# A delta-rule attention feeding an MLP: weights and joins in another order, chunk 0's moves ahead of a block read, chunk 1's second update two pieces later

## The chip, the cores and the metric

The kernel runs on one core of one Trainium2 chip. The metric is the device time of one execution in microseconds (us), and of several executions the median. Besides, one execution of each kernel is recorded by the hardware profiler; all durations of single instructions come from that one.

## What is computed

Two stages, joined by a transposition. The first is the delta rule: per batch and head (4 and 8 of them) a 48 × 48 state is read and corrected token by token, over 768 tokens. The second is an MLP on the 3,072 rows of 384 values that this gives: a product with `w_in` (384 × 2048), x · sigmoid(x), and a product with `w_out` (2048 × 384). All is float32.

```python
for t in range(S):                      # B, H, S, D = 4, 8, 768, 48
    kt, vt, bt = k_n[:, :, t], v[:, :, t], beta[:, :, t, None]     # k_n: keys of length 1
    y[:, :, t] = einsum('bhd,bhde->bhe', q[:, :, t], state)
    v_old = einsum('bhde,bhd->bhe', state, kt)
    state = state + bt[..., None] * einsum('bhd,bhe->bhde', kt, vt - v_old)
...
x = y.transpose(0, 2, 1, 3).reshape(B * S, H * D)
h = x @ w_in
out = (h * (1 / (1 + exp(-h)))) @ w_out
```

## The kernel before

**The tiling.** The 768 tokens are cut into six chunks of 128 and each chunk into two halves of 64. For a half, the token-by-token recurrence becomes a small triangular system for each batch and head: scores of keys against keys and queries against keys, the inverse of a 64 × 64 triangle, a product with the corrected values, an update of the state, and the outputs. The inverse is built from 32 × 32 blocks, which VectorE inverts in 31 steps for all batches and heads at once ("rank", L628). The blocks go out to DRAM and come back in that other layout: the read is `block_in` (L581–583), whose tile is `g`. Then TensorE joins two 32 × 32 inverses to a 64 × 64 one, in many products of 32 × 32: a "corner" (L718), a "turned" product (L734), a "straight" one (L747) and a "merge" (L807). Each of these is done for batches 0 and 1 and for batches 2 and 3.

**The names in the trace.** `pt` (L501) is a transposition of keys or queries on TensorE (four for one batch), evacuated by VectorE or ScalarE. `pa` (L530) are scores; VectorE's mask (L540, `above`) evacuates those of queries. `pl`, `px` and `py` belong to the joins. `ph` (L829) and `pz` (L841) are the steps before the update `pu` (L861). `pyc` (L909 and L922) holds the outputs of a half, one bank for batches 0 and 1 (g = 0) and one for batches 2 and 3 (g = 1). `phid` (L1049) is the hidden layer of the MLP, and `po`, `px` and `py` at L1084 and L1156 its output.

**From outputs to the MLP.** `even_heads` (L930 on) brings a `pyc` bank into the layout of `xT`, where heads and their 48 values lie along the 128 partitions. Every bank is copied once as a whole to `part` (48 × 512). The even heads are then copied from `pyc` to `xT`, six copies of 48 × 128 for each bank, on ScalarE (`by_act`, L545) or VectorE (`by_dve`, L548). The odd heads need other partitions and go from `part` to `xT` by DMA; these are the "moves", collected in a list and issued on SyncE's queue by `move()` (L902). The first phid of a half waits for all of them.

**The MLP's pieces.** The MLP is written as a list of pieces. A piece of the hidden layer is a *run*: six matmuls of 128 × 128 by 128 × 256 into half of a `phid` bank. `run(n)` issues the next n pieces. A run needs its slab of `w_in` (256 columns) narrowed to the type that the products use; `fill` ("f") issues a narrowing, which is spread over ScalarE (L232), VectorE (L237, L241) and POOL (L245).

**The loads.** The DMAs that SyncE issues stand in one list (`line`), which keeps the order of the program. A slab of `w_in` is three DMAs of 256 KB (`fetch_w_in`, L278–293). `deep(...)` makes a load wait until the last but one DMA of the list has landed, so that two are under way at a time. The raw slabs go to rooms that are free at that time. Slab 7 goes into `sums_of_g`, where the queries of chunk 1 lie until they are transposed.

**The order of the work.** Each engine executes in program order, and the program order of everything around the change is written by hand: a text of words (the call of `script`, L1549), read from left to right. A letter stands for a step and the number behind it for how often:

| word | step |
|---|---|
| `s` | next step of `solve(0)`, then of `solve(1)` |
| `j` | next piece of the joins of half 1 (`rest`) |
| `T`, `q` | transposition of chunk 1's keys, queries of the next batch |
| `r`, `f` | run of the MLP; narrowing of the next slab of weights |
| `p` | next step of `prepare(1)`: scores of chunk 1 and their blocks' way out and back |
| `i` | next steps of the inverse of chunk 1's blocks (VectorE) |
| `b`, `e`, `l`, `m`, `t`, `w`, `W` | begin a narrowing early; lengths of keys of chunk 1 (`l`) and chunk 2 (`m`); sums of weights; fetches of weights |

Behind the text a loop over the chunks (L1553 on) takes the rest: for c = 1 it ends `solve(1)`, then goes through `prepare(2)`, whose first step are the 16 transpositions of chunk 2's keys, with runs between the steps.

`solve(0)` ends with the update and the outputs of the second half, the copies to `xT` (`copy_out`) and the moves. `solve(1)` ends with `made(1, 1)`: update, outputs, moves and copies of the second half.

Of the kernel before, what the change touches and what calls it, by code (L numbers as in the profile page):

```python
# [19 lines left out]
def kernel(  # L20
# [10 lines left out]
    nc = tc.nc  # L31
    B, H, S, D = q.shape
# [8 lines left out]
    T = 32  # L41
# [48 lines left out]
    def in_line(dma):  # L90

        if line:
            behind(dma, line[-1])
        if pace or depth:
            behind(dma, pace.pop() if pace else line[-2], Sync)
        line.append(dma)
        return dma
# [12 lines left out]
    def together(*parts):  # L110
        for _ in zip_longest(*parts):
            pass
# [63 lines left out]
    def deep(fetch, *args):  # L176

        depth.append(True)
        fetch(*args)
        depth.pop()  # L180
# [397 lines left out]
                ap[rows].rearrange("s u h t -> s (u h) t")[:, :, cols], c == 0 and j % 2 == 1,  # L578
            )

    def block_in(c):  # L581
        there, g, _ = blocks[c]
        in_line(nc.sync.dma_start(out=g, in_=there[:]))

# [313 lines left out]
    def move():  # L900
        for to, of in moves:
            in_line(nc.sync.dma_start(out=to, in_=of))  # L902
        moves.clear()
# [13 lines left out]
    def new(c, g, hf):  # L917

        py = pys.pop(g)
        for u, p, e, _, _, to in of_heads():  # L920
            rows = on(e, hf, g)
            yield pin(nc.tensor.matmul(  # L922
                py[to, C * p + W * u : C * p + W * (u + 1)], lhsT=zbuf[rows, g * HB + u, hf, p, 0:D],
                rhs=aps[c, g][1][rows, u, 2 * p + e, :], start=False, stop=True, skip_group_check=True,
            ))
        copies.append(even_heads(c, g, hf, py))
        go(copies[-1])
# [3 lines left out]
    def even_heads(c, g, hf, py):  # L931

        xT, half = x_half(c, g, hf)
        if g == 0:
            parts[c, hf] = work.tile([P, 2, NP, C], FP32, name="part", tag="x", bufs=1)
        part = parts[c, hf][:, g]
        by = by_dve if c == 1 and hf == 0 and g == 1 else by_act
        by(part[0:D], py[0:D].rearrange("p (a t) -> p a t", a=NP))
        if c == 0:
            yield  # L940
        for h in chained(range(1, H, 2), range(0, H, 2)):
            if c > 0 and h == 0:
                yield
            f = D * h
            while f < D * (h + 1):
                n, at = min(D * (h + 1) - f, P - f % P), W * (1 - h % 2) + f - D * h
                while h % 2 == 0 and (n > T and at % W or f % P % W and n > T):
                    n = T
                to = xT[f % P : f % P + n, f // P, half]
                if h % 2 == 1:  # L950
                    if g == 1:
                        moves.append((
                            xT[f % P : f % P + n, f // P].rearrange("p (g t) -> p g t", g=2),
                            parts[c, hf][at : at + n, :, h // 2, :],
                        ))
                else:
                    by(to, py[at : at + n, C * (h // 2) : C * (h // 2 + 1)])
                f += n
        yield

    def copy_out():
        together(copies.pop(0))
# [18 lines left out]
    def solve(c):  # L981

        if c == 0:
            together(inner(0, 0, 0, CC))
            together(inner(0, 1, 0, M))
            yield
            first_outputs(0)
            yield
            first_outputs(1)
            yield  # L990
            together(update(0, 0, 0), update(0, 1, 0))
            yield
            together(keys(0, 0, 1), keys(0, 1, 1))
            yield
            together(inner(0, 0, 1), old(0, 0, 1))
            yield
            together(inner(0, 1, 1), old(0, 1, 1))
            yield
            together(update(0, 0, 1), update(0, 1, 1))
            yield  # L1000
            together(new(0, 0, 1), new(0, 1, 1))
            copy_out()
            copy_out()
            move()
            yield
            return
        together(merge(c, 0, False), merge(c, 1, False))
        yield
        together(keys(c, 0, 0), keys(c, 1, 0))
        yield  # L1010
        together(merge(c, 0, True), merge(c, 1, True))
        yield
        for hf in range(2):
            if hf == 1:
                together(keys(c, 0, 1), keys(c, 1, 1))
                if c > 1:
                    follow(c)
                yield
            for g in range(2):
                together(inner(c, g, hf), old(c, g, hf))  # L1020
            if hf == 1:
                if c == 1:
                    follow(c)
                load_v(c + 1)
            yield
            made(c, hf)
            yield
            copy_out()
            if hf == 0:
                yield  # L1030
# [184 lines left out]
    def feed_forward(c, hf):  # L1215

        yield from hidden(c, hf)
        yield from combine(c, hf)
# [126 lines left out]
        first_score(b)  # L1345
    busy(1)
    fetch_w_in(2)
    deep(load_q, 1)
    fetch_w_in(4)
    deep(fetch_w_in, 3)  # L1350
    deep(fetch_w_in, 6)
    deep(fetch_w_in, 5)
    begin(("in", 0))
    inv = invert_first(step)

# [82 lines left out]
    def prepare(c):  # L1438

        def evacuate(j, e, to, of):  # L1440
            if j == 1:
                mask(to, of)
            else:
                by_act(to, of)

        def scored(b):
            if b == 0:
                block_room(c)
            score(c, b, (0, 1), (A, CC), evacuate)
            if b % HB == 1:  # L1450
                block_out(c, b // HB)

        if in_blocks(c):
            for g in range(2):
                size(c, g)
            if c == 2:
                yield
                for b in range(B):
                    turn(c, b, 0, (A, CC)[b % 2], True)
            for g in range(2):  # L1460
                for b in range(HB * g, HB * (g + 1)):
                    turn_blocks(c, b, 1)
                yield
            for b in range(B):
                scored(b)
            block_in(c)
            yield
            return
        block_room(1)
        for b in range(B):  # L1470
            score(1, b, (0,), (CC, CC), evacuate)
            if b % HB == 1:
                block_out(1, b // HB)
            yield
        block_in(1)
        yield
        for b in range(B):
            score(1, b, (1,), (A, CC), evacuate)
            yield
# [67 lines left out]
                pieces = chained(feed_forward(1, 0), feed_forward(1, 1))  # L1547

    for text in (  # L1549
        "s f s f T f q T s q T j5 j4 j8 j8 f j5 f q r T j20 j5 j8 j4 j16 j5 j4 b r q r f j4 j4 f W7 r b j4 f2 j4 j4 j32 r f e j6 j6 b j8 j4 f j4 j20 f j4 r j4 j99 l h f2 b l s w2 f r2 l p r s l w3 r p r l p f l2 f l3 b l f l2 s l f l p l3 r l3 s l f l r l2 p f s2 l2 H f l4 f r2 f p2 v l g G r i p i p f r i r i2 r i r i b l i r f r i r b r2 i b b b i2 r2 i2 f b i5 r6 f r f r i2 r2 f r i r f r f i4 f i b r2 i3 b f b f r i r i f k r f r z i b r s r2 t z s b r2 b s m2 r5 t f t m f t m2 r s t m r b s b m r m2 s r m r m r c m2 s m r m t b m2 s m2 b m f m2 t r t m3 r m s m",  # L1550
    ):
        script(text)
    for c in range(1, NCH):  # L1553
        if c > 1:
            solving = solve(c)
            for n in range(9):
                go(solving)
                run(((2, 2, 2, 2, 1, 1, 2, 2, 2), (2, 2, 2, 1, 1, 2, 2, 2, 2))[c == NCH - 1][n])
                if n == 5:
                    pieces = chained(pieces, feed_forward(c, 0), feed_forward(c, 1))  # L1560
        assert next(solving, 0) == 0
        go(long_2, 99)
        if c + 1 < NCH:
            ready = prepare(c + 1)
            for _ in range(3 if c == 1 else 2):
                go(ready)
                run(2)
            step = block_steps(c + 1)
            go(ready)
            run(8 if c > 1 else 6)  # L1570
            for n, _ in enumerate(invert(c + 1, step)):
                run(int(n % 4 != 3 and n != 24))
                if n == 3:
                    load_k(c + 2)
                    if in_blocks(c + 2):
                        load_blocks(k, c + 2, ALL)
            after = lengths(c + 2) if c + 2 < NCH else iter(())
            for _ in range({1: 8, NCH - 2: 10}.get(c, 10)):
                run()
                go(after, 4)  # L1580
            go(after, 99)
# [31 lines left out]
```

## Time and profile before

| | |
|---|---|
| three runs | 639.70, 640.12 and 642.98 us; median 640.12 |
| the profiled execution | 646.08 us, of which the span of the trace is 644.3 |
| mean granted clock of TensorE in it | 0.973 |
| TensorE's matmuls | 623.5 us, 97% of the span |
| VectorE, ScalarE, GpSimd (POOL) | 401.2, 217.2 and 94.3 us |
| costliest group | phid, L1049: 1152 matmuls, 259.6 us |

How to read it: the busy share of an engine is a mean over stages. TensorE ("PE") executes matmuls and weight loads ("PEld") in two overlapping streams. The view by lines gives, for each group of like instructions, the busy time, the mean of one in ns, and the idle time ahead of the group with what ended it ("<-"). "issue" stands for time in which an engine waited for nothing that the profile shows. The view by time gives rows of consecutive like instructions: start (us from the span's start), length, engine, line, operation, tiles and shapes, and in brackets the wait ahead. The view by windows gives, for each stretch, its length, the busy time and count of PE, PEld, DVE, ACT and POOL, the granted clock of TensorE (1 is full speed), the share of time that the DMA engines are busy, and the GB/s that they move.

### The profile page before, as it was taken

Reading aid. Unit: us, or ns where it says so; the run is one execution under the profiler, and the core shown is the slowest. Engines: PE = TensorE matmul, PEld = TensorE weight load, DVE = VectorE, ACT = ScalarE, POOL = GpSimd, SP = SyncE. Lnnn points to the kernel's source line nnn. Section 1 sums busy time; section 2 is a strip of 40 time slices with the busy share of each in tenths; the row PEclk is TensorE's granted clock in tenths of the full one; section 3 lists DMA queues with packets and bytes.
Section 4 is the critical chain, followed back from the end, with each engine's and each line's share of the span. In section 5 each row is a group of like instructions: output and inputs, shape, how many; then the busy total and the mean of one; then the engine's idle time right before and its main releaser. Section 6 shows DMA issues by size and latency. Waiting matters only on the chain.

```text
span 644.3 us, 21893 instructions
## 1 busy us (share of the span) xinstructions
PE 623.5 (97%) x9642; PEld 550.1 (85%) x9642; DVE 401.2 (62%) x917; ACT 217.2 (34%) x512; POOL 94.3 (15%) x96
## 2 busy tenths in 40 slices
PE   6879999999999999999999999999999999999997
PEld 4677787756789988999989989989989989889997
DVE  5845688988865986563987563987464974212112
ACT  2655656151342122451122451122451122441120
POOL 5332630237011020010020010020001000000000
PEclk9759799999999999999999999999999999999999
DMA  9755445170278433268434268334173033100101
GB/s 190 164 141 163 146 97 132 50 148 3 58 150 145 62 85 50 54 133 136 70 79 55 47 137 138 69 79 56 26 154 76 9 79 48 40 14 1 25 0 25
DMA packets 141695, 53.69 MB, mean 83 GB/s; under 512 B 113296, under 2 KB 135056, under 8 KB 141600
## 3 DMA queue, kind: packets, MB, share of 16 engines
q1 hardware_dynamic: 141264, 52.14, 40.2%
q8 instruction: 76, 1.25, 0.8%
q10 hardware_dynamic: 336, 0.15, 0.1%
q14 instruction: 19, 0.16, 0.1%
HBM read 39.62 MB, written 10.49 MB: 78 GB/s over the span
## 4 chain that ended last, share of the span: by engine, by line
PE 92%; DMA 2%; issue 2%; DVE 1%; ACT 1%; SPq 1%; POOL 0%; DVEq 0%; POOLq 0%
PE phid L1049 39%; PE px L1156 16%; PE py L1156 12%; PE po L1084 7%; PE pa L530 3%; PE pz L841 2%; PE ph L829 2%; PE pyc L922 2%; PE pu L861 2%; PE pyc L909 2%; PE pt L501 1%; DMA kb<-in_k_dram 1%; DMA xT<-part 1%; PE px L783 1%; PE py L783 1%
## 5 line engine op out<-in xcount | busy, mean ns | idle before, releaser
L1049 PE MATMUL phid<-xT,w_in 128*128 128x256 f32 x1152 | 259.6, 383 | 2.5 <-DMA xT<-part 1.5
L1049 PEld LDWEIGHTS phid<-xT,w_in 128*128 128x128 f32 x1152 | 217.2, 191 | 33.6 <-issue 4.1
L1059 ACT ACTIVATE gT<-phid 128x512 f32<-128x512 f32 x88 | 52.6, 598 | 147.1 <-PE phid L1049 138.5
L628 DVE SCALAR_TENSOR_TENSOR rank<-g,step,x 128x31 f32<-128x31 f32 (+15 forms) x124 | 49.7, 401 | 36.9 <-DMA g<-blocks 33.4
L1138 DVE TENSOR_TENSOR sums_of_g<-gT 128x384 f32<-128x384 f32 (+1 forms) x60 | 29.8, 516 | 56.5 <-ACT gT L1059 46.0
L1156 PE MATMUL py<-w_out,sums_of_g 128*128 128x192 f32 x320 | 56.8, 329 | 0.0
L1156 PE MATMUL px<-sums_of_w,sums_of_g 128*128 128x192 f32 x320 | 56.6, 329 | 0.0
L1156 PEld LDWEIGHTS px<-sums_of_w,sums_of_g 128*128 128x128 f32 x320 | 52.2, 190 | 0.5
L1156 PEld LDWEIGHTS py<-w_out,sums_of_g 128*128 128x128 f32 x320 | 52.2, 190 | 0.4
L633 DVE TENSOR_TENSOR x<-x,rank 128x31 f32<-128x31 f32 (+15 forms) x124 | 42.5, 343 | 4.3
L468 POOL TENSOR_TENSOR vf<-vf,n_slot 128x768 f32<-128x768 f32 x10 | 14.9, 1490 | 167.9 <-DMA vf<-in_v_dram 121.8
L868 DVE TENSOR_TENSOR state<-state,pu 48x384 f32<-48x384 f32 x44 | 24.3, 552 | 21.9 <-PE pu L861 20.9
L545 ACT COPY xT<-pyc 48x128 f32<-48x128 f32 (+2 forms) x126 | 32.7, 260 | 1.7
L489 DVE STREAM_TRANSPOSE kq<-stage 128x512 f32<-128x512 f32 x28 | 28.2, 1112 | 3.9 <-DMA stage<-in_q_dram 3.8
L1156 PE MATMUL px<-sums_of_w,gT 128*128 128x192 f32 x160 | 28.4, 329 | 0.0
L1156 PE MATMUL py<-w_out,gT 128*128 128x192 f32 x160 | 28.4, 329 | 0.0
L1156 PE MATMUL px<-w_out,gT 128*128 128x192 f32 x160 | 28.0, 327 | 0.0
L841 PEld LDWEIGHTS pz<-vf,xi 64*64 64x64 f32 x768 | 25.2, 142 | 3.2 <-issue 2.6
L551 POOL COPY g<-x 64x256 f32<-64x256 f32 x4 | 5.0, 1242 | 152.5 <-DVE x L636 152.5
L1156 PEld LDWEIGHTS px<-w_out,gT 128*128 128x128 f32 x160 | 26.4, 190 | 0.6
L841 PE MATMUL pz<-vf,xi 64*64 64x48 f32 x768 | 26.9, 226 | 0.0
L1156 PEld LDWEIGHTS py<-w_out,gT 128*128 128x128 f32 x160 | 26.1, 190 | 0.3
(197 smaller groups left out, 831.1 us busy)
## 6 DMA issues: line engine op xcount, KB each, us to landing
vf<-in_v_dram SPq DMA_DIRECT2D x48, 96.0 KB, 3.1
out_dram<-o SPq DMA_DIRECT2D x42, 96.0 KB, 2.2
w_out<-in_moe_w_in_dram SPq DMA_DIRECT2D x12, 256.0 KB, 3.5
sums_of_w<-in_moe_w_out_dram SPq DMA_DIRECT2D x8, 384.0 KB, 4.4
blocks<-ap SPq DMA_DIRECT2D x40, 64.0 KB, 1.9
g<-blocks SPq DMA_DIRECT2D x5, 512.0 KB, 3.7
kb<-in_k_dram SPq DMA_DIRECT2D x12, 192.0 KB, 4.4
kb<-in_k_dram SPq DMA_DIRECT2D x24, 96.0 KB, 4.5
```

The source lines that it names most:

```text
L489: pin(nc.vector.transpose(out=kqs[c, b][:, :, j, :].rearrange("p a (i m) -> p a m i", i=T), in_=src.rearrange("p a (m d) -> p a m d", d=D) ...
L530: pin(nc.tensor.matmul(pa[e][half, p * n * W : (p + 1) * n * W], lhsT=kq[rows, p, 0, half], rhs=kq[rows, p, js[0] : js[-1] + 1, half], sta ...
L545: return pin(nc.scalar.copy(to, of))
L628: pin(nc.vector.scalar_tensor_tensor(out=tv, in0=g[:, 0:m, m : m + 1].to_broadcast([P, m, n]), scalar=step[:, m : m + 1], in1=x[:, m : m + ...
L633: yield pin(nc.vector.tensor_tensor(out=x[:, 0:m, m:T], in0=x[:, 0:m, m:T], in1=tv, op=ALU.add))
L841: yield pin(nc.tensor.matmul(pz[rows, n * D : (n + 1) * D], lhsT=xis[g][rows, u * H + 2 * p + e, :], rhs=vfs[c][rows, hf, g * HB + u, p, : ...
L868: pin(nc.vector.tensor_tensor(out=to, in0=to, in1=by_heads(pu[of]), op=ALU.add))
L1049: pin(nc.tensor.matmul(ph[:, j * GT : (j + 1) * GT], lhsT=w_in[:, a, (2 * f + j) * P : (2 * f + j + 1) * P], rhs=xTs[c, hf][:, a, :], star ...
L1059: pin(nc.scalar.activation(out=hidden_of(c, hf, f), in_=ph[:], func=ACTF.Silu, scale=-0.5 if in_blocks(c) else 0.5))
L1084: pin(nc.tensor.matmul(pos[i][:, 0:DM], lhsT=hidden_of(0, hf, f // 2)[:, at : at + C], rhs=w_outs[f // HFF][:, f % HFF, :], start=(f == 0) ...
L1138: pin(nc.vector.tensor_tensor(out=sums_of_g[:, k, fs], in0=of[0], in1=of[1], op=op))
L1156: pin(nc.tensor.matmul(to, lhsT=at, rhs=quarter(f, *b) if isinstance(b, tuple) else sums_of_w[b][:, f], start=start and f == 0, stop=f == ...
```

## The change

It has three parts.

1. **Weights' and joins' order.** Slab 3 is fetched ahead of chunk 1's queries and slab 4 behind them, with the "deep" wait, and 4, 5, 6 follow in that order. In the text, chunk 1's key transpositions (`T`) come first and its query transpositions (`q`) later; a run stands among the last joins (`j4 r j16` where there was `j20`); some runs and narrowings change places; the last `s` of the text goes.
2. **Chunk 0's moves and factors.** In the last step of `solve(0)` the moves are issued ahead of the copies. The read of the factors' blocks (`block_in(1)`) goes from `prepare(1)` to that place, and from SyncE's queue to ScalarE's. For chunk 0 the six even-head copies of the second bank go to VectorE, and the list of moves is complete before the first of these copies.
3. **Chunk 1's second update.** The step that was the text's last `s`, `made(1, 1)`, now comes behind two more runs. The two runs that stood between the first step of `prepare(2)` (nothing for TensorE) and its 16 key transpositions go in exchange, so that these transpositions stand directly behind the outputs.

The diff, with the text of words cut to the places that differ:

```diff
-    def block_in(c):
+    def block_in(c, by_scalar=False):
         there, g, _ = blocks[c]
-        in_line(nc.sync.dma_start(out=g, in_=there[:]))
+        issue(g, there[:], by_scalar)
...
         by = by_dve if c == 1 and hf == 0 and g == 1 else by_act
         by(part[0:D], py[0:D].rearrange("p (a t) -> p a t", a=NP))
-        if c == 0:
-            yield
+        if c == 0 and g == 1:
+            by = by_dve
         for h in chained(range(1, H, 2), range(0, H, 2)):
-            if c > 0 and h == 0:
+            if h == 0:
                 yield
...
             together(new(0, 0, 1), new(0, 1, 1))
+            move()
             copy_out()
             copy_out()
-            move()
+            block_in(1, True)
...
     fetch_w_in(2)
+    deep(fetch_w_in, 3)
     deep(load_q, 1)
-    fetch_w_in(4)
-    deep(fetch_w_in, 3)
-    deep(fetch_w_in, 6)
-    deep(fetch_w_in, 5)
+    for i in (4, 5, 6):
+        deep(fetch_w_in, i)
...
-        block_in(1)
         yield
...
-        "s f s f T f q T s q T j5 j4 j8 j8 f j5 f q r T j20 j5 j8 j4 j16 j5 j4 b r q r f j4 j4 f W7 r b
+        "s f s f T f T s T j5 j4 j8 j8 f j5 f r T q j20 j5 j8 j4 j16 j5 q j4 b r q r f j4 j4 q f W7 r b
...
-         j4 j20 f j4 r j4 j99 l h f2 b l s w2 f r2 l p r
+         j4 j4 r j16 f j4 r j4 j99 l h f2 b l s w2 f r l p r
...
-         g G r i p i p f r i r i2 r i r
+         g G r i p i p r2 f i i2 r i r
...
-         t r t m3 r m s m",
+         t r t m3 r m2",
...
+        if c == 1:
+            run(2)
+            go(solving)
         assert next(solving, 0) == 0
...
             ready = prepare(c + 1)
-            for _ in range(3 if c == 1 else 2):
+            if c == 1:
+                go(ready)
+            for _ in range(2):
                 go(ready)
                 run(2)
```

`issue` (L97–104) starts a DMA from ScalarE, pinned to its place among ScalarE's instructions, or appends it to SyncE's list.

More of the change, by code (lines that the diff above doesn't have):

```diff
@@ L1549 @@
     for text in (
-        "s f s f T f q T s q T j5 j4 j8 j8 f j5 f q r T j20 j5 j8 j4 j16 j5 j4 b r q r f j4 j4 f W7 r b j4 f2 j4 j4 j32 r f e j6 j6 b j8 j4 f j4 j20 f j4 r j4 j99 l h f2 b l s w2 f r2 l p r s l w3 r p r l p f l2 f l3 b l f l2 s l f l p l3 r l3 s l f l r l2 p f s2 l2 H f l4 f r2 f p2 v l g G r i p i p f r i r i2 r i r i b l i r f r i r b r2 i b b b i2 r2 i2 f b i5 r6 f r f r i2 r2 f r i r f r f i4 f i b r2 i3 b f b f r i r i f k r f r z i b r s r2 t z s b r2 b s m2 r5 t f t m f t m2 r s t m r b s b m r m2 s r m r m r c m2 s m r m t b m2 s m2 b m f m2 t r t m3 r m s m",
+        "s f s f T f T s T j5 j4 j8 j8 f j5 f r T q j20 j5 j8 j4 j16 j5 q j4 b r q r f j4 j4 q f W7 r b j4 f2 j4 j4 j32 r f e j6 j6 b j8 j4 f j4 j4 r j16 f j4 r j4 j99 l h f2 b l s w2 f r l p r s l w3 r p r l p f l2 f l3 b l f l2 s l f l p l3 r l3 s l f l r l2 p f s2 l2 H f l4 f r2 f p2 v l g G r i p i p r2 f i i2 r i r i b l i r f r i r b r2 i b b b i2 r2 i2 f b i5 r6 f r f r i2 r2 f r i r f r f i4 f i b r2 i3 b f b f r i r i f k r f r z i b r s r2 t z s b r2 b s m2 r5 t f t m f t m2 r s t m r b s b m r m2 s r m r m r c m2 s m r m t b m2 s m2 b m f m2 t r t m3 r m2",
     ):
```

## The prediction

> **What bounds the kernel now.** I read the page first (how busy each engine is), then what TensorE waited for, then equal windows with the granted clock, then the order in time around each wait. The page:
>
> ```profile
> span 644.3 us, 21893 instructions
> PE 623.5 (97%) x9642; PEld 550.1 (85%) x9642; DVE 401.2 (62%) x917; ACT 217.2 (34%) x512; POOL 94.3 (15%) x96
> q8 instruction: 76, 1.25, 0.8%
> ```
>
> PE is busy for 623.5 of 644.3 us and the change takes no matmul away, so only two things can be won: PE's idle time (20.8 us) and time at a halved clock. The profiled execution took 646.08 us, 1.8 more than its span and 0.9% more than the median of 640.12; I make the sum against 646.08 and carry the difference over to the median. The waits of PE from 40 to 110 us:
>
> ```profile
> PE px L807 <- issue: 1.6, 1, 1.6
> PE phid L1049 <- DMA xT<-part: 1.3, 1, 1.3
> PE pl L734 <- DVE xe_y L548: 0.8, 1, 0.8
> ```
>
> "issue" says that no semaphore explains the wait. The page's instruction queue has an explanation: 1.25 MB in 76 packets are 16.4 KB each, and 19,284 matmuls and weight loads over 76 are 254 per packet. I count PE's instructions in the built order (a product is two loads and two matmuls, a transposition one and one, a semaphore instruction one). The wait at L734, though the view names VectorE, and the wait at px stand 512 apart, two packets of 256. So I read both as PE having run past the end of its fetched line of instructions. [...]
>
> The clock, in windows of 3.41 us:
>
> ```profile
> 45.72:49.13 3.41, 3.41 (x65) 3.29 (x64) 1.72 (x3) 1.55 (x3) 0.00 (x0) 0.50 0.55 174
> 49.13:52.55 3.42, 3.42 (x124) 2.97 (x124) 2.35 (x3) 2.63 (x5) 1.85 (x1) 1.00 0.49 167
> 66.20:69.61 3.41, 1.82 (x45) 1.56 (x42) 2.24 (x4) 3.05 (x6) 1.35 (x1) 1.00 0.14 48
> 69.61:73.03 3.42, 3.42 (x111) 2.71 (x113) 1.26 (x3) 1.87 (x4) 1.26 (x2) 0.50 0.57 151
> 73.03:76.44 3.41, 3.41 (x35) 2.78 (x28) 3.32 (x7) 2.84 (x4) 3.41 (x5) 0.50 0.66 204
> 76.44:79.85 3.41, 3.41 (x48) 2.47 (x47) 2.38 (x4) 1.22 (x3) 2.46 (x3) 1.00 0.38 115
> ```
>
> (The number behind the POOL column is the granted clock.) The window with the 1.6 us wait has PE busy for 1.82, and the two behind it run at 0.50. That is the dearest place that the change touches.
>
> **Part 1, weights' and joins' order.** PE around that wait, then three full-clock rows for comparison:
>
> ```profile
> 63.93 1.56 PE L1049 MATMUL phid<-xT,w_in 128*128 128x256 f32 x6
> 65.42 0.75 PE L747 MATMUL pl<-sums_of_w 32*32 32x32 f32 x64
> 68.33 0.28 PE L807 MATMUL px<-xi,xe_y 32*32 32x32 f32 x6 [1.59 <-issue]
> 68.53 1.91 PE L1049 MATMUL phid<-xT,w_in 128*128 128x256 f32 x6
> 70.37 1.71 PE L807 MATMUL px<-xi,xe_y 32*32 32x32 f32 x56
> 72.01 1.53 PE L861 MATMUL pu<-z,kb 64*48 64x48 f32 x64
> 73.47 4.31 PE L1049 MATMUL phid<-xT,w_in 128*128 128x256 f32 x12
> ```
> ```profile
> 59.21 0.60 PE L501 MATMUL pt<-ident,sums_of_g 128*128 128x128 f32 x4
> 176.01 2.86 PE L1049 MATMUL phid<-xT,w_in 128*128 128x256 f32 x12
> 178.80 0.94 PE L861 MATMUL pu<-z,kb 64*48 64x48 f32 x64
> ```
>
> The built order moves one run of six phid matmuls from behind pu to between the straight joins (L747) and the merge (L807).
> - The line's border stays at its place in the count, now six instructions before the end of the merge. PE comes there one run later (63.93 to 65.42 is 1.49), while the line comes as before. Of the 1.59 I take **1.4 gained** (bounds 0.4, if the line itself is later by one, and 1.6).
> - With a run in each window PE doesn't fall to 1.82 busy, so the clock should stay. At full rate the first phid run costs 1.56 (−0.35), px by its nearest equal form (L747, 0.75 for 64) 0.66 (−1.05), pu 0.94 (−0.59), the double run 2.86 (−1.45): 3.44. The narrowing on ScalarE, VectorE and POOL must keep up with an earlier PE; I leave 0.4 for that and take **3.0 gained** (bounds 0 and 3.44).
> - Two query transpositions slide behind the 0.8 us wait at L734. Ahead of it they were free, since the line came when it came; behind it they are added. At 0.60 less the overlap of 0.16 that such a row shows with its neighbours: **0.9 lost** (bounds 0, 0.9).
> - The straight join's first bank is now the one that the second turned join has just left (the rotation of the three "a" banks moved with the transpositions), so PE waits for that evacuation:
>
> ```profile
> 61.38 0.36 ACT L545 COPY xe_y<-pl 32x256 f32<-32x256 f32 x1 [0.80 <-PE pl L734]
> ```
>
> 0.36 and the hand-over at both ends, some 0.1: **0.5 lost** (0 to 0.6; a run stands behind PE, none before it).
> - SyncE's queue: slab 3 goes ahead of the six query loads, and slab 4 now waits its turn like the others. The loads, and the first query transposition:
>
> ```profile
> 31.54 8.01 SPq L142 DMA_DIRECT2D sums_of_g<-in_q_dram  x6
> 48.27 1.03 PE L501 MATMUL pt<-ident,sums_of_g 128*128 128x128 f32 x4
> ```
>
> Even one slab's time later, the queries (issued by 39.55 today) come before that transposition, which itself moves behind the first phid run: no cost; if the cover went, one transposition's wait. But a slab now travels from 31.5 us on, while PE runs the short products of the first joins and needs its lines. No row of before has that pairing. Lower bound: a gain of 0.8, if the line at L734 comes sooner in exchange; upper: a loss of px's 1.6 on two lines, 3.2. I take **0.5 lost**, nearer to the row at L734. The last slab (W7) overwrites the queries and waits for their later transpositions; all narrowing before its own covers that, and if not, one run waits (1.5).
>
> **Part 2, chunk 0's moves and factors.** The rows of ScalarE, SyncE, VectorE and PE:
>
> ```profile
> 92.53 1.06 ACT L545 COPY part<-pyc 48x512 f32<-48x512 f32 x2 [2.79 <-PE pyc L922]
> 93.62 3.26 ACT L545 COPY xT<-pyc 48x128 f32<-48x128 f32 x12
> 94.78 0.34 SPq L583 DMA_DIRECT2D g<-blocks  x1
> 95.17 4.13 SPq L902 DMA_DIRECT2D xT<-part  x5
> 101.54 0.67 PE L1049 MATMUL phid<-xT,w_in 128*128 128x256 f32 x2 [1.33 <-DMA xT<-part]
> ```
> ```profile
> 95.93 1.42 DVE L540 TENSOR_TENSOR ap<-pa,above 128x256 f32<-128x256 f32 x4 [0.29 <-PE pa L530]
> 97.99 1.16 PE L530 MATMUL pa<-stage 48*64 48x64 f32 x64
> 167.96 1.85 DVE L548 COPY xT<-pyc 48x128 f32<-48x128 f32 x6
> ```
>
> The five moves need only part (done at 93.59). Today they stand behind the factors' read, which SyncE holds until the blocks have landed, at 94.78. Put first they start at about 93.65 instead of 95.17, 1.52 earlier, more than PE's 1.33: **1.33 gained** (0 if a later queue entry holds them, 1.33).
> Six of the twelve xT copies go to VectorE, 1.85 by the row of chunk 1. They stand before the masks (L540), which free the banks of the second pair of scores: masks end at 97.35 + 1.85 = 99.2 where pa wants its third bank at 98.0 and its fourth at 98.6; counted mask by mask, **0.4 lost** (0 to 1.85).
> The factors' read goes behind ScalarE's six copies: 93.62 + 1.63 = 95.25, 0.5 later, and the inverse's chain on VectorE starts about 0.9 later. Its end has cover:
>
> ```profile
> 135.25 2.04 DVE L606 STREAM_TRANSPOSE xe_y<-sums_of_w 128x1024 f32<-128x1024 f32 x1
> 141.22 0.47 PE L783 MATMUL py<-xe_y,ap 32*32 32x32 f32 x33
> ```
>
> The transposition ends at 137.29 and PE comes at 141.22: 3.9 us, so I cost this at nothing; if the cover went, it would cost up to 0.9. ScalarE itself has 1.63 less to copy and one issue more (0.34 by SyncE's row).
>
> **Part 3, chunk 1's second update.** Two runs move ahead of update (pu) and outputs (pyc), and the 16 transpositions stand directly behind them.
>
> ```profile
> 182.02 2.53 PE L1049 MATMUL phid<-xT,w_in 128*128 128x256 f32 x11 [0.97 <-issue]
> 184.39 1.91 PE L501 MATMUL pt<-ident,kb 128*128 128x128 f32 x16
> 180.74 1.06 ACT L545 COPY part<-pyc 48x512 f32<-48x512 f32 x2 [2.54 <-PE pyc L922]
> 181.83 3.26 ACT L545 COPY xT<-pyc 48x128 f32<-48x128 f32 x12
> ```
>
> The line that was late by 0.97 now begins in pyc, with two runs before it. This wait, too, is at a line's border (3,838 instructions behind the one at px, 15 lines less two). **0.97 gained** (0 to 0.97). But the third transposition group takes the bank of pyc's first half, which ScalarE empties with both part copies and six xT copies: 1.06 + 1.63 + 0.11 after pyc ends, 2.8. The first eight transpositions last 8 × 0.109 = 0.87, of which 0.16 overlap pyc's tail: **2.1 lost** (1.0 to 2.1). Today two phid runs stand there and hide it. Queued behind that wait is all of PE; VectorE's evacuations are late with it, but keep 5 us of runs before the scores.
>
> **The sum.** Gained 1.4 + 3.0 + 1.33 + 0.97 = 6.7; lost 0.9 + 0.5 + 0.5 + 0.4 + 2.1 = 4.4; net 2.3: 643.8 for a profiled execution and **637.8** for the median. 0.5% is about what a measurement of this kernel can tell from no change (636.9 to 643.3 count as none).
>
> **The rivals.**
> - *The clock drops in the new row of transpositions* (the slower side). Place: 183 to 187 us, where 2.1 us of idle PE now stand between transpositions. In before, 1.59 idle in a window was enough. Price: a window at half clock under dense phid runs defers half of it, 1.7; two cost 3.4, and the result is 637.8 + 3.4 = 641.2. It decides from 1.4 windows on, where it outweighs the 2.3. For it: the idle time is longer than at px. Against it: the work around it is phid, whose first full window lifted the clock at 76.44. [...]
> - *The clock's saving isn't there*: the drop at 69.61 comes elsewhere in the joins, or the median's executions never had it (642.98 and 639.70 lie 3.3 apart, the size of one such drop). 637.8 + 3.0 = 640.8.
> - *The weight loads hold up PE's lines* at 31 to 37 us, both by 1.6 where I took 0.5: 640.5. The reverse, lines that come sooner and no loss at L734 and the masks: about 635.2.
> - *The moves aren't earlier*, since an older load holds their queue entry: 639.1.
>
> **How the numbers follow.** My sum 0.42 (636.3 to 639.3; a third of it below 636.9); the sooner lines 0.20 (634 to 636.5); no clock saving 0.20 (640 to 643.5, a fifth of it above 643.3); drop in the transpositions 0.12 (639.5 to 645, over half above 643.3 where it comes together with the case before it); late lines or late moves 0.06. Faster by over 0.5%: 0.14 + 0.20 = 0.34; slower by over 0.5%: 0.04 + 0.08 + 0.04 = 0.16; between them 0.50. The range, 634.2 to 642.9, leaves out one in ten at each end.
>
> **What would show it.** Right: no issue wait at px, the clock at 1.00 from the first phid run to the end, no wait of phid for xT<-part, and a wait of about 2 us at the second half of the transpositions for ScalarE's xT copies. Wrong: a 0.50 window behind 183 us or still in the joins, an issue wait over 2 us between 33 and 40 us, or masks (L540) that hold the scores for over 1 us.

## The result and the profile after

The changed kernel took 643.18 us (median of 22 runs, 640.42 to 646.11), the kernel before 640.35 (22 runs, 638.36 to 644.02). The medians lie 2.8 us apart. The ratio is 1.0038, 95% interval 1.0024 to 1.0052, so the changed kernel is 2.4 us slower (1.5 to 3.3) by it. I had 637.8 with an upper end of 642.9. Of 105 later runs of before, one (649.05 us) was in a slower state and isn't counted below.

The profiled executions say the opposite. That of before took 646.08 us, that of the changed kernel 643.93, 0.1 from my 643.8. The head of the page after, two lines, and its instruction queue:

```profile
span 642.1 us, 21891 instructions
PE 621.3 (97%) x9642; PEld 548.1 (85%) x9642; DVE 401.9 (63%) x923; ACT 215.8 (34%) x506; POOL 94.6 (15%) x96
q8 instruction: 76, 1.25, 0.9%
```

The profiled execution of before lies 5.7 us above the median of its kernel and above all its 22 runs; that of the changed kernel 0.75 above. So the first question is what the profiled execution of before had that others have not. The waits of TensorE in the changed kernel, from 43 to 110 us, and one from 170 to 190:

```profile
PE pa L530 <- DVE state L868: 1.2, 1, 1.2
PE pl L747 <- ACT xi L545: 0.6, 1, 0.6
PE pl L747 <- ACT xe_y L545: 0.4, 1, 0.4
PE pl L734 <- DVE sums_of_w L725: 0.4, 1, 0.4
```
```profile
PE pt L501 <- ACT xT L545: 1.8, 1, 1.8
```

The issue wait at px, the wait for `xT<-part` and the line late in phid at 181 us are gone, as forecast. The wait of the transpositions (1.8 for my 2.1) and one of the straight joins (0.4 for 0.5) are there. Two are new: the second straight join waits for ScalarE's xi (0.6), and the first scores of chunk 1 (pa) wait for VectorE's state (1.2). That addition of the update to the state empties a bank of pu which these scores take. The clock, where before it was halved:

```profile
67.28:70.69 3.41, 3.41 (x98) 2.81 (x85) 2.24 (x4) 3.23 (x7) 0.93 (x1) 1.00 0.49 167
70.69:74.10 3.41, 3.41 (x128) 2.88 (x127) 2.07 (x4) 2.35 (x5) 2.48 (x3) 1.00 0.43 125
74.10:77.50 3.40, 2.22 (x39) 1.64 (x38) 3.28 (x7) 3.09 (x6) 3.22 (x4) 1.00 0.72 250
```

It stays at 1.00 to the end of TensorE's work. But this execution isn't typical either: its mean granted clock is 0.975, where 18 of the 22 runs had 0.978 or more. Ahead of the change's stretch it had one window more at half clock. The same window in it and in experiment e1 (the kernel before once more, below), where the clock had already risen:

```profile
22.91:26.32 3.41, 3.41 (x87) 3.08 (x89) 2.99 (x13) 2.09 (x6) 0.26 (x1) 0.50 0.74 137
```
```profile
22.91:26.32 3.41, 3.16 (x110) 2.73 (x108) 3.00 (x13) 2.88 (x9) 0.46 (x1) 1.00 0.77 144
```

### The profile page after: what moved, and what is told of

Read it like the earlier page. It is cut to its first block, busy times and chain, and to the rows that moved or that the text cites. A ratio compares the mean times of both kernels' runs of the same rounds, so it can differ in the third digit from the quotient of the medians.

```text
span 642.1 us, 21891 instructions
## 1 busy us (share of the span) xinstructions
PE 621.3 (97%) x9642; PEld 548.1 (85%) x9642; DVE 401.9 (63%) x923; ACT 215.8 (34%) x506; POOL 94.6 (15%) x96
## 4 chain that ended last, share of the span: by engine, by line
PE 91%; DMA 3%; DVE 2%; issue 1%; ACT 1%; SPq 1%; POOL 0%; DVEq 0%; POOLq 0%
PE phid L1050 38%; PE px L1157 17%; PE py L1157 13%; PE po L1085 7%; PE pa L530 4%; PE pz L841 2%; PE ph L829 2%; PE pyc L909 1%; PE pyc L922 1%; PE pu L861 1%; DMA kb<-in_k_dram 1%; PE pt L501 1%; PE px L783 1%; PE py L783 1%; SPq L160 1%
## 5 line engine op out<-in xcount | busy, mean ns | idle before, releaser
L628 DVE SCALAR_TENSOR_TENSOR rank<-g,step,x 128x31 f32<-128x31 f32 (+15 forms) x124 | 49.7, 401 | 36.0 <-DMA g<-blocks 32.5
L545 ACT COPY xT<-pyc 48x128 f32<-48x128 f32 (+2 forms) x120 | 31.2, 260 | 1.6
```

The lines of the kernel that those rows point to most:

```text
L545: return pin(nc.scalar.copy(to, of))
L628: pin(nc.vector.scalar_tensor_tensor(out=tv, in0=g[:, 0:m, m : m + 1].to_broadcast([P, m, n]), scalar=step[:, m : m + 1], in1=x[:, m : m + ...
```

## The experiments

Two theories stood against each other. **A**: the clock's saving (and part of the wait at px) belonged to one execution of before; without them the losses outweigh. **B**: the drop is in most executions, and the time is lost elsewhere. Experiments e1 to e4 shared their runs of before (median 642.38, 35 runs), as did e5 to e8 (642.55) and e9 to e12 (642.67). Before's median is 2 us higher here than in the first comparison (e1 to e4 ran on one chip, e5 to e12 on another), so each run is compared with its own set. All diffs are against before unless it is said.

**e1, the kernel before once more.** No edit.

> The kernel before once more, unchanged, to see whether its profiled execution was typical. Theory A (the clock's saving of 3.0 us was a property of that one execution): the new profile has the 1.6 us issue wait at px again, but the windows behind it stay at clock 1.00; span about 639 to 641, mean granted clock 0.977 or more in most executions, median 640.3. Rival B (the drop is in most executions, and the changed kernel loses its time elsewhere): the 0.50 windows behind px come again, mean clock about 0.973, and the median stays 640.3 although the span of the profiled execution was 644.3.

Median 642.24, ratio 0.9998 (0.9976 to 1.0020). The new profiled execution has a span of 638.2 us, 6.1 shorter than the first. The page's head, TensorE's waits from 43 to 110 us, and two windows at px and behind it:

```profile
span 638.2 us, 21893 instructions
PE 618.6 (97%) x9642; PEld 546.1 (86%) x9642; DVE 401.1 (63%) x917; ACT 216.6 (34%) x512; POOL 94.9 (15%) x96
```
```profile
PE phid L1049 <- DMA xT<-part: 1.1, 1, 1.1
PE px L807 <- ACT xe_y L545: 0.4, 1, 0.4
PE pl L734 <- DVE sums_of_w L725: 0.4, 1, 0.4
```
```profile
63.86:67.28 3.42, 3.41 (x135) 2.82 (x134) 2.90 (x5) 3.34 (x7) 0.71 (x2) 1.00 0.72 235
67.28:70.69 3.41, 3.03 (x114) 2.69 (x107) 2.49 (x5) 3.36 (x8) 3.24 (x4) 1.00 0.35 68
```

The same instructions in the same order, and the issue wait at px isn't there at all, which I had not expected in either theory; nor is the 0.8 at L734. No drop of the clock follows. Theory A holds in its main point, but its wait at px and its span (639 to 641) didn't come.

How often does the drop come? Every execution has its mean granted clock. One window of 3.41 us more at half clock lowers it by 0.0027 (3.41 × 0.5 / 642). In the traces of this case 0.978 or more goes with at most eight such windows (without those behind TensorE's last product), 0.975 and 0.976 with nine, 0.973 with ten. The three traces with a drop in or behind the last joins (before, e3, e10) have 0.973; the two with nine (the changed kernel, e12) have the ninth near 24 us, ahead of the joins. Of 104 executions of before, 71 had 0.978 or more and a median of 641.67 us, and 33 had 0.976 or less and took 2.9 us longer (644.59); 7 had 0.973 or less. So the case that I had read, with ten windows, is the rare one. Where the clock was low in an execution without a trace isn't known. The price is near my 3.0, but it is 2.9 for those at 0.976 too, whose one window more can defer no more than half of 3.41; so it isn't shown to be the clock's alone.

**e2 to e4, one part each.** e2 is the order of the loads and of the words, the last `s` kept; e3 is part 2; e4 is part 3:

```diff
# e2
+    deep(fetch_w_in, 3)
     deep(load_q, 1)
-    fetch_w_in(4)
-    deep(fetch_w_in, 3)
...
-        "s f s f T f q T s q T ...
+        "s f s f T f T s T ...
# e3
...
+        if c == 0 and g == 1:
+            by = by_dve
...
             together(new(0, 0, 1), new(0, 1, 1))
+            move()
             copy_out()
             copy_out()
-            move()
+            block_in(1, True)
...
# e4
...
+        if c == 1:
+            run(2)
+            go(solving)
         assert next(solving, 0) == 0
...
```

> Part 1 alone: loads' order and the text of words (with its last s kept), the rest as before. Theory A: slower by 2 to 3 us (gained 1.4 at px; lost 0.9 for two transpositions, 0.4 to 0.9 at the straight joins, 1.2 more at the line late in L734, 1.2 for the wait of pa for VectorE's state). Rival B: faster by 1 to 3 us, by the clock, and the loss comes from parts 2 and 3.

> Part 2 alone: chunk 0's moves first, the factors' read by ScalarE, six copies by VectorE. Theory A: the wait of phid for xT<-part (1.3 us) goes, nothing takes its place, 1.0 to 1.4 us faster (median about 639.2). Rival B: within 0.5 us of before, since something later is paced by another engine.

> Part 3 alone: chunk 1's second update two runs later. Theory A: a wait of 1.8 us of the key transpositions for ScalarE's xT copies comes, the issue wait of 1.0 us in phid goes or moves: slower by 0.8 us (0.5 to 1.8). Rival B (the idle time there drops the clock in some executions): slower by 2 to 4 us, with a mean clock lower by 0.003 or more in those executions.

e2: 645.30, ratio 1.0049 (1.0024 to 1.0074). e3: 642.78, 0.9999 (0.9974 to 1.0023). e4: 643.23, 1.0007 (0.9986 to 1.0028). The loss is in part 1, which I had as the part that gains most. e3 lost its wait for `xT<-part`, and its profiled execution met px and the dropped clock; e4 met px without the drop:

```profile
PE px L807 <- issue: 2.1, 1, 2.1
...
65.17:68.58 3.41, 1.27 (x27) 1.04 (x21) 1.99 (x4) 2.82 (x5) 1.67 (x1) 1.00 0.64 203
68.58:72.00 3.42, 3.42 (x88) 2.62 (x90) 0.81 (x2) 1.39 (x4) 0.45 (x2) 0.50 0.65 165
```
```profile
PE px L807 <- issue: 1.1, 1, 1.1
...
65.47:68.88 3.41, 2.36 (x107) 2.10 (x94) 2.69 (x5) 3.31 (x7) 0.79 (x1) 1.00 0.76 224
```

With e5 (below), five profiled executions have the joins in before's order: the issue wait at px was 1.6, 0, 2.1, 1.1 and 0 us (before, e1, e3, e4, e5). For e4 rival B is out: the mean clock of its executions (0.978) is that of before, and its trace has the 1.8 us wait that theory A named.

**e5 to e8, the parts of part 1.** e5 has the order of the loads alone (the diff's hunk at L1346); e6 the `T` and `q` of the text alone; e7 the run among the joins alone, with the runs behind it that give one up or change places; e8 is the changed kernel with `T` and `q` as before.

```diff
# e6
-        "s f s f T f q T s q T j5 j4 j8 j8 f j5 f q r T j20 j5 j8 j4 j16 j5 j4 b r q r f j4 j4 f W7 ...
+        "s f s f T f T s T j5 j4 j8 j8 f j5 f r T q j20 j5 j8 j4 j16 j5 q j4 b r q r f j4 j4 q f W7 ...
# e7
...
-        j4 j20 f j4 r j4 j99 l h f2 b l s w2 f r2 l p r
+        j4 j4 r j16 f j4 r j4 j99 l h f2 b l s w2 f r l p r
...
-        i p f r i r i2 r i r
+        i p r2 f i i2 r i r
...
```

> Of part 1 the order of the loads alone (slab 3 ahead of the queries, slabs 4 to 6 with the deep wait). Theory A (the loss of part 1 is in the transpositions' place, which rotates the banks and adds two transpositions to the stretch from 58 to 72 us): within 1 us of before, the stretch from the second corrected product (pz) to the end of chunk 0's outputs as long as before, 43.8 us. Rival C (the loads slow the lines and the narrowing): 2 to 3 us slower, with narrowing or loads named as releasers of waits in the joins.

> Of part 1 the order of the key and query transpositions alone. Theory A: 1.5 to 2.5 us slower; the waits of the straight joins for ScalarE (xe_y 0.4, xi 0.6) are there, and each query transposition behind the first phid runs adds 0.6. Rival C: within 0.7 us of before, no such waits.

> Of part 1 the run among the last joins alone, with the two shifted runs that follow from it in the text. Theory A: the issue wait at px goes (at most 1.6, less in most executions), and the wait of chunk 0's third scores (pa) for VectorE's state comes (0.5 to 1.2 us), since a run less stands behind pu: 0 to 1 us slower. Rival C: faster by 1 to 3 us, as the prediction had it for the clock and the line.

> The changed kernel with the transpositions of keys and queries in the order of before. Theory A: 1.5 to 2.5 us faster than the changed kernel, so about 0 to 1 us slower than before. Rival C: as slow as the changed kernel, 2.8 us slower than before.

e5: 642.89, ratio 1.0014 (0.9987 to 1.0041). e6: 643.80, 1.0017 (0.9993 to 1.0041). e7: 641.59, 0.9990 (0.9963 to 1.0018). e8: 643.61, 1.0017 (0.9998 to 1.0037). No interval leaves out 1; e6 and e8 come out at 1.1 us where 1.5 to 2.5 and 0 to 1 were expected. These runs mix executions of different clock. Among those at 0.978 or more alone, of the run and of its own set of before, the means differ by (a split made after the runs; the intervals are worked out from their scatter):

| run | slower by, us (95% interval) |
|---|---|
| e2, part 1 | 3.1 (1.7 to 4.6) |
| e3, part 2 | −0.4 (−1.7 to 0.8) |
| e4, part 3 | 0.7 (−0.1 to 1.6) |
| e5, loads | 0.0 (−1.2 to 1.2) |
| e6, transpositions | 1.8 (0.6 to 3.0) |
| e7, run in the joins | −0.1 (−1.2 to 0.9) |
| e8, all but transpositions | 1.0 (0.1 to 2.0) |
| e9, the changed kernel again (below) | 2.4 (1.4 to 3.4) |

So with the clock left out the change loses 2.4, and of its parts only the place of the transpositions is slower beyond its interval. e6 lies in its range of 1.5 to 2.5, and the five parts (e3 to e7) add up to 2.0.

The traces show where the transpositions' place costs. The stretch from the first of the corrected products (pz, first start) to chunk 0's last output (pyc, last start) holds the same 1,230 matmuls in every kernel. The rows by line of e1, e6, e8 and the changed kernel, "first to last start":

```profile
L841 PE MATMUL pz<-vf,xi x64: 303/303/338, 43.1 to 46.5; 64*64 64x48 f32 x64
L922 PE MATMUL pyc<-ap,z x64: 216/216/218, 86.0 to 86.9; 64*48 64x64 f32 x64
```
```profile
L841 PE MATMUL pz<-vf,xi x64: 303/303/338, 42.8 to 46.1; 64*64 64x48 f32 x64
L922 PE MATMUL pyc<-ap,z x64: 216/216/218, 88.3 to 89.2; 64*48 64x64 f32 x64
```
```profile
L841 PE MATMUL pz<-vf,xi x64: 303/303/338, 42.2 to 45.5; 64*64 64x48 f32 x64
L922 PE MATMUL pyc<-ap,z x64: 216/216/218, 86.8 to 87.7; 64*48 64x64 f32 x64
```
```profile
L841 PE MATMUL pz<-vf,xi x64: 303/303/338, 43.3 to 46.7; 64*64 64x48 f32 x64
L922 PE MATMUL pyc<-ap,z x64: 216/216/218, 89.9 to 90.7; 64*48 64x64 f32 x64
```

| kernel | transpositions moved | run moved | the stretch, us | of it at half clock, us |
|---|---|---|---|---|
| e1, e4, e5 | no | no | 43.8, 44.9, 45.2 | 3.7, 3.9, 5.0 |
| e7, e8, e12 | no | yes | 45.2, 45.5, 45.8 | 3.6, 5.0, 6.8 |
| e6 | yes | no | 46.4 | 6.5 |
| e2, changed, e9, e11 | yes | yes | 47.4, 47.4, 47.5, 47.6 | 4.3, 6.9, 6.5, 5.8 |

(The executions with the drop have 48.9, 49.7 and 53.2: e3, before, e10.) The stretch begins at half clock, for longer in one execution than in the other, and that can account for up to half of the difference: for 1.2 of the 1.8 between e6 and the first row. e2 has as much half clock as e7 and e8 and is 2.0 longer; so the moved transpositions cost 0.6 to 2 us by the traces. The moved run's 0.7 is within the 1.4 between like traces, and e7's times don't show it. e6 and e2 have the waits of both straight joins, e7 and e8 the wait of pa for the state (1.0) and not px; these waits come with the edits.

**e9 to e12, undoing the waits.** e9 is the changed kernel once more. In e10, against the changed kernel, a word `A` moves the rotation of the three "a" banks on by one, ahead of both straight joins and once behind. e11 is e10 with the update's step (`s`) ahead of two reductions (`l`). e12 is before with part 2, e7's first edit and the same exchange of `s` and `l`.

```diff
# e10, against the changed kernel
...
+            elif what == "A":
+                A.rotate(-1)
...
-        b r q r f j4 j4 q f W7 r b j4 f2 j4 j4 j32 r f e j6 j6 b ...
+        b r q r f j4 A j4 q f W7 r b j4 f2 j4 j4 j32 r f e A j6 A j6 b ...
# e11 besides, and e12
-        l h f2 b l s w2
+        l h f2 b s l w2
...
```

> The changed kernel once more, unchanged, as the measure for the next two on the same chip. Theory A: 2 to 3 us slower than before; waits of about 0.4, 0.6, 1.0 and 1.8 us (straight joins for ScalarE's xe_y and xi, pa for VectorE's state, pt for ScalarE's xT) as in its first profile.

> The changed kernel with the rotation of the three a banks moved on by one ahead of both straight joins (and once more behind them), so that no join meets a bank that was left just before. Theory A: the waits of 0.4 and 0.6 us go, 0.6 to 1.0 us faster than the changed kernel. Rival (TensorE only waits later, for VectorE's evacuations or state): the two waits go, the wait of pa grows by as much, same time.

> The same, and VectorE's addition to the state ahead of two reductions of key lengths (1.08 us) that stood before it. Theory A: the wait of pa for the state goes as well (1.0 us), so 1.6 to 2.0 us faster than the changed kernel, within 1 us of before. Rival: the wait comes back at the next product that needs the state or the lengths, at most 1 us faster.

> The kernel before with what should pay alone: chunk 0's moves first (0.6 to 1.3 us gained), the run among the last joins (0.5 to 1.5 gained on average, by the issue wait at px) and VectorE's state ahead of the two reductions (so that the run's cost, the 1.0 us wait of pa, isn't paid). Theory A: 1 to 2.5 us faster than before. Rival (a run in the joins moves the issue wait elsewhere): within 0.7 us of before.

e9: 644.83, ratio 1.0017 (0.9993 to 1.0041), with the same waits (0.4, 0.6, 1.1 and 1.8). This second set of the changed kernel doesn't exclude no change by its ratio, though its medians lie 2.2 apart; at like clock it does (2.4). e10: 645.24, 1.0028 (1.0002 to 1.0054). e11: 646.12, 1.0056 (1.0032 to 1.0080). e12: 642.82, 0.9997 (0.9972 to 1.0022). Here theory A fails: to take the waits away gains nothing. The rivals are right that no time is saved; that e11 is 1.9 slower than e9 at like clock (0.2 to 3.6) was in none of them, and its cause is open. TensorE's waits of e10, then e11, then e12, from 43 to 110 us:

```profile
PE px L807 <- ACT xi L545: 1.3, 1, 1.3
PE pa L530 <- DVE state L868: 1.2, 1, 1.2
PE pl L718 <- issue: 1.1, 1, 1.1
PE pl L734 <- issue: 0.8, 1, 0.8
```
```profile
PE px L807 <- ACT xi L545: 1.4, 1, 1.4
PE phid L1050 <- POOL w_in L245: 0.7, 1, 0.7
PE pa L530 <- DVE vf L834: 0.6, 1, 0.6
```
```profile
PE phid L1050 <- POOL w_in L245: 0.7, 1, 0.7
PE pa L530 <- DVE vf L834: 0.6, 1, 0.6
```

In e10 both waits of the straight joins go (0.4 + 0.6), and the merge waits 1.3 for ScalarE's copies. Its trace is of its second slowest execution of 12 and has two issue waits besides; e11's is of its fastest. In e11 and e12 the wait for the state (1.0 to 1.2) shrinks to 0.2 or goes, and TensorE waits 0.6 for the reductions' successor, the corrected values (vf), and 0.7 for a narrowing. The reading that fits is that ScalarE and VectorE hold the pace here, and the order chooses at which product TensorE meets them; no run made these engines faster to test it. A rival is the clock: 6 of 12 executions of e10 and 8 of e11 had 0.976 or less, and 2 of e9. At like clock, too, e10 isn't faster than e9 (2.9 against 2.4 behind before). e12, the parts that should pay alone, doesn't pay measurably.

## Why the prediction was wrong

The step that failed is **"I make the sum against 646.08 and carry the difference over to the median"**. It moves a difference between two kernels over to executions that don't have what makes it. Among executions at a mean clock of 0.978 or more, whose traces show no such drop, the change loses 2.4 us (e9), most of it by the place of the transpositions (e6, 1.8).

- **px, "1.4 gained".** Right in place: no trace with the moved run shows the 1.6 us at px. But in before it is 1.6, 0, 2.1, 1.1 and 0 by execution, on average 1.0; without the two that have the drop, 0.4.
- **The clock, "3.0 gained".** Right for the execution that I read, wrong as a rule. It was 33 of 104 executions of before and 6 of 34 of the changed kernel that had 0.976 or less: 32% to 18%, times 2.9 us, is 0.4, an estimate, since so few executions don't establish that difference. The rival with this name had 0.20. Two signs were there: the first three runs of before lie 3.3 us apart, which I quoted, and its profiled execution (646.08) lies 3.1 above the slowest of them (642.98), so that it can't be what the median measures.
- **Two transpositions, "0.9 lost"; the bank, "0.5 lost".** The bank's wait is 0.4 as forecast, but the rotation brings the second straight join on a bank just left too (0.6). Together with the transpositions 1.8 us at like clock (0.6 to 3.0) for my 1.4: 1.0 of it are these waits, but e10, without them, isn't faster, so how the rest is lost is open.
- **Loads, "0.5 lost".** Nothing can be put down to them. The issue wait at L734 around 33 us is 2.5 and 2.2 in two executions of the changed kernel, but 1.3 and 2.6 in two of before, 2.0 in e5, and e5 is 0.0 slower at like clock:

```profile
PE pl L734 <- issue: 1.3, 1, 1.3
```
```profile
PE pl L734 <- issue: 2.6, 1, 2.6
```
```profile
PE pl L734 <- issue: 2.5, 1, 2.5
```

  (before, e1 and the changed kernel). One execution of each kernel would have made a loss of 1.2 of it.
- **Not foreseen: pa waits 1.1 to 1.2 for VectorE's state.** I wrote that the engines "must keep up with an earlier PE" and left 0.4 for narrowing. One run less between pu and pa was enough for 1.0 (e7). VectorE in the changed kernel:

```profile
72.88 1.02 DVE L237 TENSOR_SCALAR w_in<-w_in 128x768 uint32<-128x768 uint32 x1
73.82 1.08 DVE L389 TENSOR_REDUCE ss<-sq 128x8 f32<-128x384 f32 x2
74.94 2.27 DVE L868 TENSOR_TENSOR state<-state,pu 48x384 f32<-48x384 f32 x4
```

```profile
76.20 0.69 PE L530 MATMUL pa<-stage 48*64 48x64 f32 x30 [1.18 <-DVE state L868]
```

  A narrowing, two reductions and the additions to the state stand behind each other without a gap, from 72.88 to 77.21, while TensorE has one run between pu and pa. In before it has two, in the profiled execution at half clock besides, and they hid that queue. In time e7 is no slower for it (−0.1), since its wait at px goes.
- **Moves, "1.33 gained".** The wait goes (0.4 in e9, 0 in the other six traces with part 2). In traces with the moves as before it was 1.3, 1.1, 0.6, 1.0, 0.2, 0 and 1.3 (before, e1, e2, e4, e5, e6, e7), on average 0.8; so about 0.7. **Masks, "0.4 lost"**: no wait for them in any trace's list from 92 to 112 us.
- **The late line in phid, "0.97 gained"**: gone with part 3; in the eight traces without part 3 it is 0.2 to 1.5, on average 0.8. **The transpositions' wait, "2.1 lost"**: 1.8 in each trace that has part 3. The rival that the clock drops there came in none of the six:

```profile
179.92:183.33 3.41, 1.75 (x61) 1.44 (x52) 3.32 (x6) 2.48 (x8) 0.00 (x0) 1.00 1.06 174
183.33:186.74 3.41, 3.22 (x19) 2.97 (x20) 2.58 (x5) 2.29 (x8) 0.00 (x0) 1.00 0.75 140
```

  PE is busy for 1.75 there, no more than the 1.82 at px, and the next window is at 1.00 (these two are the changed kernel's).

The sum with what was measured: gained 1.0 + 0.4 + 0.7 + 0.8 = 2.9; lost 1.8 + 1.1 + 1.8 = 4.7; 1.8 slower, inside 1.5 to 3.3. The last 1.0 to the medians' 2.8 isn't assigned and may be scatter. That the profiled time came out at 643.93 for my 643.8 is luck: that execution had one window more at half clock near 24 us, which isn't in my sum, and against the wait of pa (1.2), the second bank (0.6) and 1.2 more at L734 stand masks, loads and the transpositions, each with an error of its own.

## What to carry to other kernels

Before a difference of a few us is worked out from one profiled execution, set its time beside the median of the others: if it lies outside their range, look for a term (a wait without a releaser, a halved clock) that is that execution's own, and weigh such a term by how often it comes, not by its size. Where the engines behind TensorE stand in queues without gaps, an edit that ends one wait can be paid at the next (in e10 waits of 0.4 and 0.6 us went and one of 1.3 came): compare the length of a whole stretch, between two products that both kernels have, with as much of it at half clock, and not the list of waits. Where every execution has its mean clock, compare executions of like clock first: here that told the parts apart where the medians didn't. A rotation of banks is part of the order: what is inserted between two allocations decides who meets whose evacuation (here the straight joins that of xe_y, 0.4 us, and of xi, 0.6).

## What the runs showed of the hardware

**An issue wait is a matter of the execution.** One and the same code waited 1.6 us at px in one execution (before) and not at all in another (e1); at L734, around 33 us, 1.3 and 2.6. That they stand at borders of fetched lines is my reading of their places; no run tests it. In the trace of before 254 matmuls and 255 weight loads lie between the 0.8 us wait at L734 and the wait at px, and the instruction queue moves one packet between 65.8 and 67.0 us, ahead of the end of the wait at 68.33.

**The phase of the clock's windows differs from trace to trace, and the busy time of PE in a window doesn't decide alone.** The window at px begins at 66.20 us in before and at 65.17 in e3. Windows of 3.41 us followed by 0.50 had PE busy for 1.82 (before) and 1.27 (e3), but also 2.07 and 2.32 in e10, of small products:

```profile
52.62:56.03 3.41, 2.32 (x114) 1.94 (x113) 2.38 (x6) 1.45 (x3) 0.00 (x0) 1.00 0.54 166
56.03:59.44 3.41, 3.40 (x24) 2.67 (x24) 0.39 (x1) 1.89 (x3) 1.83 (x1) 0.50 0.56 175
...
69.69:73.10 3.41, 2.07 (x46) 1.51 (x45) 1.69 (x3) 3.07 (x6) 1.82 (x1) 1.00 0.02 5
73.10:76.51 3.41, 3.41 (x54) 2.50 (x54) 0.38 (x1) 0.34 (x1) 0.00 (x0) 0.50 0.71 218
```

while the window at 179.92 above, with 1.75, kept the clock. Eight transpositions of 128 × 128 are in it:

```profile
180.58 1.09 PE L501 MATMUL pt<-ident,kb 128*128 128x128 f32 x8
```

They take 1.09 us of it, so that 0.66 of 3.41 us is left for all other matmuls of the window at 179.92, less than the 1.27 of e3 behind which the clock dropped; here it held. The mean granted clock of the 104 executions of before goes from 0.971 to 0.981. What in a window counts isn't shown.
